# Gated attention, routed experts and a feed-forward in one kernel: scaled keys and weight remainders on GpSimd, the last pair's states ahead of its scores, rows of two batches at other places

## The chip, the cores and the metric

One of the cores of a Trainium2 chip runs the kernel. The metric is the device time of one launch in microseconds (us). The engines are TensorE (PE in the rows; PEld is its weight load), VectorE (DVE), ScalarE (ACT), GpSimd (POOL) and SyncE (SP), which issues most of the transfers. Each works through its own instructions in order and waits for the others by semaphores, so the order in which the program is written is the order on each engine.

## The reference, cut to what matters

```python
for t in range(S):                         # B=4, H=8, S=768, D=48
    state = alpha[:, :, t, :, None] * state + einsum('bhd,bhe->bhde', k[:, :, t], v[:, :, t])
    y[:, :, t] = einsum('bhd,bhde->bhe', q[:, :, t], state)
x = y.transpose(0, 2, 1, 3).reshape(B * S, H * D)         # 3072 rows of 384

logits = x @ w_gate                        # 8 experts
expert_idx = argmax(logits, axis=1)
gate_w = softmax(logits)[arange(N), expert_idx]
for e in range(E):                         # every row goes to one expert
    h = maximum(x[expert_idx == e] @ w1[e], 0.0)          # 384 -> 1024
    out[expert_idx == e] = gate_w * (h @ w2[e])           # 1024 -> 384

h = out @ w_in                             # 384 -> 2048
result = (h * sigmoid(h)) @ w_out          # 2048 -> 384
```

## The kernel before, in words

The kernel has three stages in one launch: the attention with the choice of experts (to about 140 us of the profiled span), the expert layer, and the last feed-forward. Matrix products of the two later stages are made of three, since every operand is split into a rounded high part and a remainder (`wh`, `wl` of a weight slice, `xh`, `xl` of the rows, `hh`, `hl` of the hidden layer).

**Attention.** Two heads make a pair, four pairs a batch row b, so there are pairs p = 0 to 15, and the loop at line 986 has an epilogue p = 16. The sequence is cut in six chunks of 128. Within a chunk the decay is taken out of the recurrence: the queries are multiplied by a running product of alpha, the keys by one from the other end. This preparation runs on "tiles" T = 0 to 12 (with the four pairs of a later batch row packed into three tiles, whose spare rows GpSimd's DMAs gather into the buffer `E_136`, line 518). Its five steps are closures of `prep` (line 525): P_SCAN (`f0`, lines 533 and 536, VectorE), Q_SCALE (line 545, GpSimd for T > 0), DECAY (line 540, ScalarE), R_SCAN (`f1`, line 551, VectorE, into `Rv`, which has one buffer) and K_SCALE (`f2`, line 556, VectorE, reads `Rv`). A table places them: P_SCAN of the tile of pair p at place "scan" of pair p-2, R_SCAN at "end" of pair p-2, K_SCALE at "head" of pair p-1.

A pair itself is: scores of three chunks (line 578, PSUM tile `Ap` in two banks, used again for the other three), the mask (line 583, VectorE, frees `Ap`), keys transposed (line 566, copied to `kst` by ScalarE, line 569), products with the states of the pair before (line 635, tile `Yp`), scores 3 to 5, state updates `U` (lines 590 and 597), the products within the chunks of the pair before (lines 647 and 650, added to `Yp`), the scan over states (`So`, line 607, VectorE), its copies into `Sb` (line 624 ScalarE, 622 VectorE), and copies of `Yp` into `xb` (`y_copy`, line 667 ScalarE, 665 VectorE). `warm(n)` is n products on a tile of zeros (line 506), whose result nobody reads.

**Choice of experts, beside the pairs.** After a batch row, `beside_pairs` (line 920) spreads its routing over the places A, F1, F2, F3, C1 and C2 of the next pairs: logits, `choose` and `weigh` (the gate), `ranks`, `slots`, `digits`, `hots`, `invert`, `add`, which turn the choice into a table of row numbers, and `rows` (line 879), which transposes 128 rows on TensorE, scales them on ScalarE (line 888, tile `xr`, four buffers) and writes them to `x_d` in HBM. The routing of the last batch row cannot hide there: its logits come after pair 15 (line 683, tile `Lp`).

**Expert stage.** The first expert is taken in two parts. Its first 192 rows (`CA`) are gathered from the first three batch rows, so `F1(t)` and `S1(t)` (line 1172 and 1201), t = 0 to 7, run while the routing of the last batch row is done; then the row numbers `gidx` are known (line 842), GpSimd gathers the rest of the rows (line 344), `x_tile` transposes them (line 354) and splits them (lines 356 and 357), and F1 of the second part follows. Between the steps t, the lists `beside` and `between` place the rest of the routing and `rows`. Weight slices arrive by SP (line 319) and are split by `w_split`: ScalarE rounds (`wh`, line 330), VectorE subtracts (`wl`, line 331). All later experts and the last feed-forward follow.

## Time and profile before

| | us |
|---|---|
| median of 3 runs | 793.6 |
| lowest and highest run | 791.74, 795.31 |
| profiled execution | 796.22 |
| its span, first to last instruction | 794.5 |
| PE busy in the span | 768.5 (97%) |
| DVE busy | 479.1 (60%) |
| ACT busy | 358.4 (45%) |
| POOL busy | 147.2 (19%) |

The profiled execution is one run of its own, 2.6 us above the median of the runs; 1.7 us of it lie outside the span. The timeline rows give the start in the span, the duration, the engine and the line; in brackets stands how long the engine was idle before, and what ended that. The windows give the busy time of the engines in stretches and the granted clock of TensorE (1.00 is full speed, 0.50 half).

### The profile page before, as it was taken

The page shows a single profiled execution, that of the slowest core. Times are in us where ns is not written, and L with a number is a line of the kernel's source. Part 1 is how long each engine was busy: PE and PEld are TensorE (multiplying, and loading weights), DVE is VectorE, ACT ScalarE, POOL GpSimd, SP SyncE. Part 2 cuts the span into 40 slices and gives each one's busy share as a digit, 9 for nine tenths or more (in the row PEclk, how much of TensorE's full clock was granted, in tenths as well). Part 3 has the DMA queues.
Part 4 walks back from the last instruction along what each step waited for, and adds up shares of the span by engine and source line. Part 5 has one row for each costly group of instructions (what it writes and reads, how often), then busy time and mean ns, then how long its engine had stood idle before and what let it go on. Part 6 is the DMA issues. An engine that isn't in the chain of part 4 may idle for free.

```text
span 794.5 us, 13324 instructions
## 1 busy us (share of the span) xinstructions
PE 768.5 (97%) x5088; PEld 699.0 (88%) x5088; DVE 479.1 (60%) x825; ACT 358.4 (45%) x680; POOL 147.2 (19%) x194
## 2 busy tenths in 40 slices
PE   7999998899999999999999999999999999999995
PEld 5878877899899999999888999989889988999994
DVE  8989976747788887788688433333433333333332
ACT  2456554425445455556544334453544444333231
POOL 4445321131332231311121200020020011002002
PEclk9899999999999999999999999999999999999998
DMA  9878893433554554555210110031022000001001
GB/s 235 213 181 229 195 268 116 140 115 120 172 170 151 187 186 156 188 179 171 89 60 18 48 45 18 0 93 35 1 75 52 19 11 31 1 1 41 1 1 44
DMA packets 41642, 80.54 MB, mean 101 GB/s; under 512 B 5640, under 2 KB 19863, under 8 KB 41568
## 3 DMA queue, kind: packets, MB, share of 16 engines
q1 hardware_dynamic: 37568, 67.56, 28.9%
q0 software_dynamic: 4000, 12.03, 5.1%
q8 instruction: 42, 0.69, 0.4%
q14 instruction: 32, 0.26, 0.1%
HBM read 68.03 MB, written 9.44 MB: 97 GB/s over the span
## 4 chain that ended last, share of the span: by engine, by line
issue 42%; PE 40%; DVE 5%; DMA 5%; POOL 4%; ACT 2%; SPq 1%; POOLq 0%; DVEq 0%; ACTq 0%
PE hp L1172 16%; PE both L1201 9%; PE yb L1201 4%; POOL out_dram L1386 3%; PE Ap L578 2%; PE both L1367 1%; PE ob L1367 1%; DMA x_d<-xr 1%; PE xt L354 1%; PE Yp L635 1%; DVE Pf L533 1%; PE Yp L650 1%; SPq L437 1%; DMA a__825<-in_alpha_dram 1%; PE Lp L683 1%
## 5 line engine op out<-in xcount | busy, mean ns | idle before, releaser
L1172 PE MATMUL hp<-xh,wh 128*128 128x512 f32 (+9 forms) x504 | 184.7, 369 | 0.1
L1172 PE MATMUL hp<-xh,wl 128*128 128x512 f32 (+9 forms) x504 | 183.7, 368 | 0.8 <-DVE wl L331 0.8
L1346 DVE TENSOR_TENSOR sg<-hp,sg 128x512 f32<-128x512 f32 (+1 forms) x97 | 66.5, 686 | 159.5 <-ACT sg L1345 155.0
L1172 PE MATMUL hp<-xl,wh 128*128 128x512 f32 (+9 forms) x504 | 131.2, 368 | 0.0
L1345 ACT ACTIVATE sg<-hp 128x512 f32<-128x512 f32 (+1 forms) x97 | 57.6, 594 | 156.6 <-PE hp L1172 155.8
L1172 PEld LDWEIGHTS hp<-xh,wh 128*128 128x128 f32 x504 | 94.7, 188 | 10.6 <-issue 0.4
L1172 PEld LDWEIGHTS hp<-xl,wh 128*128 128x128 f32 x504 | 91.7, 188 | 13.9
L1172 PEld LDWEIGHTS hp<-xh,wl 128*128 128x128 f32 x504 | 94.8, 188 | 10.1 <-DVE wl L331 1.0
L1355 DVE TENSOR_TENSOR hl<-sg,hh 128x512 fp32r<-128x512 f32 x95 | 65.8, 692 | 61.8 <-PE ob L1367 41.2
L1354 ACT CAST hh<-sg 128x512 fp32r<-128x512 f32 x95 | 59.0, 621 | 71.1 <-DVE sg L1346 71.1
L1181 ACT ACTIVATE hh<-hp 128x192 fp32r<-128x192 f32 (+8 forms) x72 | 34.5, 479 | 115.2 <-PE hp L1172 113.2
L1386 POOL DMA_INDIRECT out_dram<-o,sidx x24 | 24.2, 1007 | 323.3 <-ACT o L1383 318.6
L1099 POOL TENSOR_TENSOR wl<-dx,wh 128x384 fp32r<-128x384 f32 x32 | 37.9, 1184 | 196.4 <-ACT wh L1096 196.4
L331 DVE TENSOR_TENSOR wl<-raw,wh 128x768 fp32r<-128x768 f32 x64 | 62.1, 972 | 11.4 <-ACT wh L330 10.7
L1367 PE MATMUL both<-wh,hh 128*128 128x384 f32 x190 | 64.4, 339 | 0.0
L1367 PE MATMUL both<-wh,hl 128*128 128x384 f32 x190 | 64.2, 338 | 0.0
L1367 PE MATMUL both<-wl,hh 128*128 128x384 f32 x190 | 64.0, 337 | 0.0
L1367 PE MATMUL ob<-wh,hl 128*128 128x384 f32 x190 | 63.5, 334 | 0.0
L1367 PE MATMUL ob<-wh,hh 128*128 128x384 f32 x190 | 63.5, 334 | 0.0
L1367 PE MATMUL ob<-wl,hh 128*128 128x384 f32 x190 | 63.5, 334 | 0.0
L1183 DVE SCALAR_TENSOR_TENSOR hl<-hp,hh 128x192 fp32r<-128x192 f32 (+8 forms) x72 | 38.9, 540 | 38.7 <-ACT hh L1181 37.5
L330 ACT CAST wh<-raw 128x768 fp32r<-128x768 f32 x64 | 52.9, 828 | 0.3 <-DMA raw<-in_wt_dram 0.3
(359 smaller groups left out, 1464.9 us busy)
## 6 DMA issues: line engine op xcount, KB each, us to landing
raw<-in_wt_dram SPq DMA_DIRECT2D x64, 384.0 KB, 3.2
raw<-in_w_dram SPq DMA_DIRECT2D x32, 384.0 KB, 2.7
raw<-in_alpha_dram SPq DMA_DIRECT2D x16, 336.0 KB, 3.5
x_d<-xr SPq DMA_DIRECT2D x24, 192.0 KB, 2.0
E<-in_q_dram SPq DMA_DIRECT2D x18, 144.0 KB, 4.2
E<-in_k_dram SPq DMA_DIRECT2D x18, 144.0 KB, 3.3
E<-E POOLq DMA_DIRECT2D x18, 114.0 KB
E<-in_q_dram SPq DMA_DIRECT2D x4, 336.0 KB, 10.8
```

Of the source, the lines that this page charges most:

```text
L330: nc.scalar.copy(hi, raw[t])
L331: eng.tensor_tensor(lo, raw.pop(t), hi.bitcast(F32), op=ALU.subtract)
L1099: nc.gpsimd.tensor_tensor(r["lo"], r["x"], r["hi"].bitcast(F32), op=ALU.subtract)
L1172: nc.tensor.matmul(hp, lhsT=a[:, kc * 128 : (kc + 1) * 128], rhs=x[:, kc, c0:c1], start=(i == 0), stop=(i == 8))
L1183: nc.vector.scalar_tensor_tensor(hl[:, :n], in0=hp, scalar=0.0, in1=hh[:, :n].bitcast(F32), op0=ALU.max, op1=ALU.subtract)
L1201: nc.tensor.matmul(yb[dc][:, c0:c1], lhsT=a[:, c : c + 128], rhs=b_[:, : c1 - c0], start=(f == 0 and i == 0), stop=(f == NF - 1 and i == 2),)
L1345: nc.scalar.activation(sg[:, z], hp[:, z], AF.Sigmoid)
L1346: nc.vector.tensor_tensor(sg[:, z], hp[:, z], sg[:, z], op=ALU.mult)
L1354: nc.scalar.copy(hh[:, z], sg[:, z])
L1355: nc.vector.tensor_tensor(hl[:, z], sg[:, z], hh[:, z].bitcast(F32), op=ALU.subtract)
L1367: nc.tensor.matmul(yb[tt], lhsT=a[:, tt * 128 : (tt + 1) * 128], rhs=b_[:, 384:768], start=(f == 0 and i == 0), stop=(f == NF2 - 1 and i = ...
L1386: sc = nc.gpsimd.indirect_dma_start(out=out, out_offset=bass.IndirectOffsetOnAxis(ap=sidx[:, i : i + 1], axis=0), in_=ob, in_offset=None,)
```

## The change

Five places are edited. (1) K_SCALE of the tiles 3 to 6 moves from VectorE to GpSimd. (2) DECAY of tile 1 is issued later in pair 0, and pair 0 ends with 22 products on zeros instead of 6. (3) In pair 14 the rows of the last batch row but one go a place later; the first two weight splits go together to C1 of pair 15, the third to the epilogue, and the remainder of the fourth to GpSimd. (4) In pair 15 the updates and states stand before the scores 3 to 5; a copy of `Yp` of pair 14 moves to VectorE; the transposes of the first gathered tile stand before the last within-products. (5) In the expert stage `ranks`, `slots`, `digits` and `hots` follow the first two `rows` behind F1(2), the other `rows` one step later, two more remainders go to GpSimd, and `x_tile(0, 3)` follows S1(7).

```diff
             def f2():
-                nc.vector.tensor_tensor(
+
+                (nc.gpsimd if 2 < T < 7 else nc.vector).tensor_tensor(
                     s["ks"][:n], s["ks"][:n], chunks(s["Rv"][:n, 1 : SP + 1])[:, :, 1 : CH + 1], op=ALU.mult
...
             c0 = 3 * g * CH
             dst, src = xb[b][:, i, c0 : c0 + 3 * CH], st[p]["y", g].rearrange("p c t -> p (c t)")
-            if p == NP - 1 and g:
+            if p >= NP - 2 and g:
                 nc.vector.tensor_copy(dst, src)
...
                     (p, "C1"): s_["choose"] + s_["weigh"],
-                    (p + 1, "A"): [row[0], row[1]],
-                    (p + 1, "F1"): [row[2]],
-                    (p + 1, "F2"): [row[3]],
+                    (p + 1, "F1"): [row[0], row[1]],
+                    (p + 1, "F2"): [row[2], row[3]],
...
-                    (p + 2, "F1"): [lambda: w_split(0)],
                     (p + 2, "F2"): [invert, add],
                     (p + 2, "F3"): [gather_a],
-                    (p + 2, "C2"): [lambda: w_split(1), lambda: w_split(2), lambda: w_load(4)],
+                    (p + 2, "C1"): [lambda: w_split(0), lambda: w_split(1)],
+                    (p + 2, "C2"): [lambda: w_load(4)],
...
-        for i in (P_SCAN, Q_SCALE, DECAY):
+        for i in (P_SCAN, Q_SCALE):
             f(1, i)
...
             if on:
                 ks_transpose(p, 3, 5)
+            if p == 0:
+                f(1, DECAY)
...
+            if not on:
+                x_rows(XG[0], XS[0], 0, 0, 128, bank(2, [128, KD, 128], "xt"))
+
+            if p == NP - 1:
+                updates(p, 0, 5)
+                states(p)
             if on:
                 for c in range(3, 6):
                     scores(p, c)
+            if p < NP - 1:
                 updates(p, 0, 5)
             if oy:
                 within(p - 1, 0)
                 within(p - 1, 1)
-            if on:
+            if p < NP - 1:
                 states(p)
...
             if p == 0:
-                warm(6)
+                warm(22)
...
             if not on:
-                x_rows(XG[0], XS[0], 0, 0, 128, bank(2, [128, KD, 128], "xt"))
                 x_rows(XG[1], XS[0], 1, 0, CA - 128, bank(0, [128, KD, 128], "xt"))
...
-                w_split(3)
+                w_split(2)
+                w_split(3, nc.gpsimd)
...
         beside = {
-            0: row[0:2],
-            1: row[5:6],
-            2: [last["turns"], invert, add, lambda: gather(0, (1, 2, 3))],
+            1: row[0:2] + [last["ranks"]] + last["slots"] + [digits, hots],
+            2: row[5:6] + [last["turns"], invert, add, lambda: gather(0, (1, 2, 3))],
             6: [lambda: x_tile(0, 1, CA - 128)],
-            7: [lambda: x_tile(0, 2, bk=4), lambda: x_tile(0, 3, bk=3)],
+            7: [lambda: x_tile(0, 2, bk=4)],
         }
...
         for t in range(NF):
-            if t == 1:
-                for f in [last["ranks"]] + last["slots"] + [digits, hots]:
-                    f()
             if t + 1 < NF:
                 F1(t + 1, 0, CA)
+            if t in (0, 2):
+                w_split(t + 3 + (t == 0), nc.gpsimd)
             for f in beside.get(t, []):
                 f()
-            if t in (0, 2, 3, 4):
-                w_split(t + 3 + (t == 0))
+            if t in (3, 4):
+                w_split(t + 3)
             if t >= 4:
                 next_load()
-            S1(t, 0, CA, row[2:5] if t == 0 else [])
+            S1(t, 0, CA, row[2:5] if t == 1 else [])
+        x_tile(0, 3, bk=3)
         F1(*seq[0])
```

VectorE in pairs 2 to 4 before (`a__326` and `a__419` are the alphas of tiles 4 and 5, `E_135` the keys and queries of tile 4; a scan prints as SCALAR_TENSOR_TENSOR):

```order
L551 SCALAR_TENSOR_TENSOR Rv<-a__326,D_0_159 128x774
L583 TENSOR_TENSOR Am<-Ap,mask 128x768
L556 TENSOR_TENSOR E_135<-E_135,Rv 128x768
L533 SCALAR_TENSOR_TENSOR Pf<-a__419,Z_156 128x774
L536 RECIPROCAL D_1_160<-Pf 128x6
L583 TENSOR_TENSOR Am<-Ap,mask 128x768
L607 SCALAR_TENSOR_TENSOR So<-U,E_134 112x288
L551 SCALAR_TENSOR_TENSOR Rv<-a__419,D_1_160 128x774
```

and now (`a__342` and `a__435` are the same two alphas):

```order
L551 SCALAR_TENSOR_TENSOR Rv<-a__342,D_0_159 128x774
L584 TENSOR_TENSOR Am<-Ap,mask 128x768
L533 SCALAR_TENSOR_TENSOR Pf<-a__435,Z_156 128x774
L536 RECIPROCAL D_1_160<-Pf 128x6
L584 TENSOR_TENSOR Am<-Ap,mask 128x768
L608 SCALAR_TENSOR_TENSOR So<-U,E_134 112x288
L551 SCALAR_TENSOR_TENSOR Rv<-a__435,D_1_160 128x774
```

Line 556, the key scaling, is gone from this engine, and the scan of line 551 into `Rv` follows with one mask and one scan in between. It stands on GpSimd, before and now, behind the constants (lines 496 and 498 are their last):

```order
L496 MEMSET keys 128x1
L498 MEMSET caps 1x1 x8
L545 TENSOR_TENSOR E_131<-E_131,Pf 128x768
L545 TENSOR_TENSOR E_132<-E_132,Pf 128x768
L518 DMA E_136<-E_135 16x1824 x2
```

```order
L496 MEMSET keys 128x1
L498 MEMSET caps 1x1 x8
L557 TENSOR_TENSOR E_135<-E_135,Rv 128x768
L545 TENSOR_TENSOR E_131<-E_131,Pf 128x768
L557 TENSOR_TENSOR E_131<-E_131,Rv 128x768
L545 TENSOR_TENSOR E_132<-E_132,Pf 128x768
L557 TENSOR_TENSOR E_132<-E_132,Rv 128x768
L518 DMA E_136<-E_135 16x1824 x2
```

Line 557 is the key scaling there: that of tile 4 (`E_135`) comes behind the constants, and each later one behind the query scaling (line 545) of the tile after it.

VectorE at the last pair before (`E_5_136` belongs to pair 15, `Yp_1946` is the second half of its output, `wl0` to `wl2` are weight remainders):

```order
L583 TENSOR_TENSOR Am_1867<-Ap_1860,mask_163 128x768
L331 TENSOR_TENSOR wl0_97<-raw_1487,wh0_96 128x768
L838 TENSOR_TENSOR tab_108<-tab_108,pt_1880 128x32
L893 TENSOR_SCALAR gidx_a_110<-tab_108 128x2
L894 TENSOR_SCALAR fl_111<-carry_114 1x1
L583 TENSOR_TENSOR Am_1907<-Ap_1900,mask_163 128x768
L607 SCALAR_TENSOR_TENSOR So_1931<-U_177,E_5_136 112x288
L622 COPY Sb_1_162<-So_1931 48x5x48
L331 TENSOR_TENSOR wl1_99<-raw_1489,wh1_98 128x768
L331 TENSOR_TENSOR wl2_101<-raw_1588,wh2_100 128x768
L665 COPY xb_1692<-Yp_1946 112x384
```

and now (`Yp_1906` is the second half of pair 14, `Yp_1960` that of pair 15):

```order
L584 TENSOR_TENSOR Am_1883<-Ap_1876,mask_163 128x768
L839 TENSOR_TENSOR tab_108<-tab_108,pt_1894 128x32
L894 TENSOR_SCALAR gidx_a_110<-tab_108 128x2
L895 TENSOR_SCALAR fl_111<-carry_114 1x1
L608 SCALAR_TENSOR_TENSOR So_1924<-U_177,E_5_136 112x288
L623 COPY Sb_1_162<-So_1924 48x5x48
L584 TENSOR_TENSOR Am_1935<-Ap_1928,mask_163 128x768
L666 COPY xb_1708<-Yp_1906 112x384
L331 TENSOR_TENSOR wl0_97<-raw_1503,wh0_96 128x768
L331 TENSOR_TENSOR wl1_99<-raw_1505,wh1_98 128x768
L357 TENSOR_TENSOR xl0_105<-xt_1964,xh0_104 128x3x128
L666 COPY xb_1708<-Yp_1960 112x384
```

The scan `So` stands before the second mask of the pair, no remainder is left ahead of it, and the two remainders follow behind a copy of pair 14's output.

GpSimd at the start of the expert stage before (`gidx_a` are the row numbers of the first 192 rows, `gidx` those of the rest):

```order
L344 DMA xg_106<-x_d,gidx_a 128x384
L344 DMA xg_107<-x_d,gidx_a 64x384
L344 DMA xg_107<-x_d,gidx 128x384
L344 DMA xg_2025<-x_d,gidx 128x384
L344 DMA xg_2026<-x_d,gidx 64x384
```

and now:

```order
L344 DMA xg_106<-x_d,gidx_a 128x384
L344 DMA xg_107<-x_d,gidx_a 64x384
L331 TENSOR_TENSOR wl_103<-raw,wh_102 128x768
L331 TENSOR_TENSOR wl_2026<-raw,wh_2025 128x768
L331 TENSOR_TENSOR wl_2028<-raw,wh_2027 128x768
L344 DMA xg_107<-x_d,gidx 128x384
L344 DMA xg_2041<-x_d,gidx 128x384
L344 DMA xg_2042<-x_d,gidx 64x384
```

Three weight remainders stand ahead of the gathers of the first expert's other rows.

## Rows read from the trace of the kernel before

**Rows 1.** Busy time of each engine, one stretch; columns: stretch, span, busy, clock, DMA.

```profile
180.00:200.00 20.00, 20.00 (x115) 18.29 (x114) 15.27 (x31) 9.78 (x19) 3.27 (x3) 1.00 0.42 130
```

**Rows 2.** Timeline of TensorE, pairs 0 and 1; start, us, instruction, [idle before, releaser].

```profile
15.28 0.83 PE L506 MATMUL Lw<-wz 128*128 128x256 bf16 x6
18.77 1.65 PE L578 MATMUL Ap<-E 48*128 48x128 f32 x12 [2.65 <-issue]
```

**Rows 3.** TensorE in windows: span, busy, granted clock, DMA share, GB/s.

```profile
19.00:20.00 1.00, 1.00 (x11) 0.50 1.03 277
...
135.00:136.00 1.00, 1.00 (x14) 0.50 0.24 66
143.00:146.00 3.00, 1.65 (x16) 1.00 0.55 202
```

**Rows 4.** Timeline of VectorE, pairs 0 to 6.

```profile
12.63 2.30 DVE L551 TENSOR_TENSOR_SCAN Rv<-a__142,D 112x774 f32<-112x774 f32 x1
...
25.70 0.96 DVE L583 TENSOR_TENSOR Am<-Ap,mask 128x768 f32<-128x768 f32 x1 [1.09 <-PE Ap L578]
...
36.56 0.95 DVE L556 TENSOR_TENSOR E<-E,Rv 128x768 f32<-128x768 f32 x1
37.43 1.76 DVE L533 TENSOR_TENSOR_SCAN Pf<-a__419,Z 128x774 f32<-128x774 f32 x1
...
40.83 1.74 DVE L551 TENSOR_TENSOR_SCAN Rv<-a__419,D 128x774 f32<-128x774 f32 x1
...
43.34 1.48 DVE L556 TENSOR_TENSOR E<-E,Rv 128x768 f32<-128x768 f32 x1
...
53.73 0.96 DVE L583 TENSOR_TENSOR Am<-Ap,mask 128x768 f32<-128x768 f32 x1 [2.12 <-PE Ap L578]
```

**Rows 5.** Timeline of GpSimd, tiles 1 to 5.

```profile
11.66 1.64 POOL L545 TENSOR_TENSOR E<-E,Pf 112x768 f32<-112x768 f32 x1 [7.33 <-DVE Pf L533]
...
40.18 3.82 POOL L545 TENSOR_TENSOR E<-E,Pf 128x768 f32<-128x768 f32 x1
```

**Rows 6.** Instructions of line 545 on GpSimd: count, ns least, median and most.

```profile
L545 POOL TENSOR_TENSOR E<-E,Pf x12: 1625/1637/3822, 11.7 to 103.6; 128x768 f32<-128x768 f32 x9, 112x768 f32<-112x768 f32 x3
```

**Rows 7.** Timeline of ScalarE, pair 14 to the expert stage.

```profile
119.07 0.58 ACT L888 ACTIVATE xr<-Xt,gt 128x384 f32<-128x384 f32 x1 [1.05 <-DMA x_d<-xr]
...
127.06 0.35 ACT L569 COPY kst<-Tp 128x224 f32<-128x224 f32 x1 [0.70 <-PE Tp L566]
...
140.08 0.83 ACT L330 CAST wh<-raw 128x768 fp32r<-128x768 f32 x1
```

**Rows 8.** Timeline of TensorE, pair 15 to the expert stage.

```profile
128.93 0.21 PE L597 MATMUL U<-v__1586,kst 128*48 128x48 f32 x1
...
132.79 1.34 PE L635 MATMUL Yp<-E,Sb 112*112 112x128 f32 x10 [2.33 <-ACT xb L667]
...
137.79 1.95 PE L683 MATMUL Lp<-xb,wgs 112*32 112x256 f32 x24
...
144.56 0.60 PE L885 MATMUL Xt<-ident,xb 112*128 112x112 f32 x4 [1.35 <-ACT xr L888]
```

**Rows 9.** Timeline of VectorE, pair 15 to the second part.

```profile
130.96 0.76 DVE L607 TENSOR_TENSOR_SCAN So<-U,E 112x288 f32<-112x288 f32 x1 [1.41 <-PE Yp L650]
...
140.94 0.96 DVE L331 TENSOR_TENSOR wl<-raw,wh 128x768 fp32r<-128x768 f32 x1 [2.22 <-ACT wh L330]
...
145.73 0.96 DVE L331 TENSOR_TENSOR wl<-raw,wh 128x768 fp32r<-128x768 f32 x1 [0.80 <-ACT wh L330]
...
153.92 0.18 DVE L842 TENSOR_SCALAR gidx<-tt 128x32 uint32<-128x32 f32 x1
...
163.71 0.36 DVE L357 TENSOR_TENSOR xl<-xt,xh 128x192 fp32r<-128x192 f32 x1 [0.47 <-ACT xh L356]
```

**Rows 10.** Timeline of TensorE, end of the expert's first part.

```profile
162.92 0.40 PE L354 MATMUL xt<-ident,xg 64*128 64x64 f32 x3 [0.79 <-DMA xg<-x_d,gidx]
...
164.34 0.30 PE L1172 MATMUL hp<-xh,wh 128*128 128x256 f32 x1
```

More of the change, by code (lines that the diff above doesn't have):

```diff
@@ L1214, in gla_moe_kernel @@
         F1(0, 0, CA)
-        XB[0], XBS[:] = -1, [3, 4, 7, 4, 7, 4, 3, 7, 3]
+        XB[0], XBS[:] = -1, [3, 4, 7, 3, 4, 7, 4, 7, 3]
         digits, hots, invert, add = last_tb
```

## The prediction

> **What bounds the kernel now.** I read the profile from the coarse to the fine: the busy shares in windows, then the timelines of TensorE and VectorE wherever TensorE is not full, then the chain of waits through those places. From about 165 us to the end TensorE is full at the full clock: the window at 180 us shows 20.00 busy of 20 [rows 1]. Nothing of the change lies behind that point. So the edits are worth what they move the start of the second part of the first expert, which before is at 164.34 us [rows 10]; each microsecond there should come out at the end.
>
> In front of that point VectorE sets the pace of the pairs: its timeline has almost no idle time between 15 and 51 us. Its waits stand at few places: 1.09 us before the mask at 25.70 and 2.12 us before the one at 53.73 [rows 4], both for scores. TensorE waits longest before the scores of pair 1, 2.65 us [rows 2], and before the state products of pair 15, 2.33 us [rows 8]. Behind both waits its granted clock is 0.50, the lower of the two levels (1.2 GHz): in the window at 19 us and in the one at 135 us [rows 3]. Behind waits of 1.35 us, as before the transposes at 144.56 [rows 8], it stayed at 1.00, in the window at 143 us [rows 3]. The last piece, from the logits of the last batch row (end 139.74, from 137.79 + 1.95 [rows 8]) to the row numbers (end 154.10, from 153.92 + 0.18 [rows 9]) and to the gathered rows (162.92 [rows 10]), is one chain of small steps.
>
> **The change part by part.** All sums are against the profiled execution, 796.22 us; they are then taken off the median of 793.6, which is 2.6 us lower.
>
> *Products on zeros and DECAY.* Six such products take 0.83 us with their overlap, some 0.107 us each [rows 2]; sixteen more take 1.7 us and lie in TensorE's wait of 2.65 us, so they cost nothing. DECAY no longer stands ahead of the copy of transposed keys on ScalarE, which lets TensorE finish its work of pair 0 some 0.5 us earlier (estimate). The wait shrinks to 2.65 + 0.5 - 1.7 = about 1.5 us. That lies nearer the 1.35 us after which the clock held than the 2.65 us after which it fell. If the clock holds, scores and state products of pair 1 take half as long and the mask at 25.70 no longer waits: 1.1 us gained. If not, 0. Below nothing I see no way, as the zeros end before the scores are released. I take +1.1; what is late next is VectorE itself, without idle time.
>
> *K_SCALE on GpSimd.* It leaves VectorE four times, 0.87 us each from start to start (36.56 to 37.43 [rows 4]). That of tile 6 lies ahead of the 2.12 us wait at 53.73 and is worth nothing; three give 2.6 us. Against this stand three costs. First, GpSimd takes 1.64 us for the same shape where VectorE is not disturbed much, and where both engines read two inputs from SBUF, one of them stretches: the query scaling at 40.18 took 3.82 us, the VectorE scan beside the one at 11.66 took 2.30 instead of 1.74, and a K_SCALE took 1.48 instead of 0.95 [rows 4, 5]. K_SCALE on GpSimd starts when R_SCAN ends; on VectorE one mask follows (some 0.85 us, its 0.96 less the overlap with the next; its other input is in PSUM) and then P_SCAN, which reads two. If it has to stand until GpSimd is done, it loses 1.64 - 0.85 = 0.8 us for each of tiles 3 and 5. Second, R_SCAN writes the only buffer `Rv`, so that of tile T+1 now waits for K_SCALE of tile T on GpSimd; behind that wait on VectorE stand the next mask and P_SCAN, for which the scores and the query scaling wait. For most tiles it is fed in time, some 4 us after the start. But K_SCALE of tile 4 stands behind the constants on GpSimd, which end where the query scaling at 40.18 starts without idle time [rows 5], or some 39.4 with what is gained ahead. It then ends at 41.1 at the earliest, while R_SCAN of tile 5 would be ready at about 40.0 (40.83 less 0.87). That is 1.1 us lost, and 2.7 if the query scaling of tile 5, right behind it, takes another 1.64 us beside it. I take 1.4. Third, nothing else moves on GpSimd's queue but the gathers of spare rows behind K_SCALE of tile 6, which have the slack of pair 5. Sum: 2.6 - 0.8 - 1.4 - 0.8 = -0.4 us. Ends: +1.5 where only the wait behind the constants is paid, and -5.5 as worked out under the slower rival.
> The Trainium skill (GPSIMD Engine Reference, section Key points) says that GpSimd shares its SBUF interfaces with VectorE and that they contend with VectorE instructions that read two SBUF inputs. The trace agrees with it in the 2.30, 1.48 and 3.82 us above, and by that rule alone every P_SCAN here stands; without it, K_SCALE would cost only the wait behind the constants, and part (1) would gain 1.5 us.
>
> *Rows of batch row 2 in pair 14.* The fourth `xr` waits 1.05 us for its buffer, whose transfer lands at 119.07 [rows 7]. Moving rows from place A to F1 and F2 does not move that landing, and the copy of transposed keys still stands behind it on ScalarE. I take 0, with +0.5 and -0.5 as ends.
>
> *The last pair.* Before, `So` starts at 130.96 [rows 9], although the last update had ended at 129.14 (128.93 + 0.21 [rows 8]); then come its copies and the state products at 132.79. Now the updates stand ahead of the scores: the keys are in place at 127.41 (127.06 + 0.35 [rows 7]), TensorE is free of the state products of pair 14 shortly after, and `So` can start at about 128.2. With its copies (the same 1.83 us from 130.96 to 132.79) less the ScalarE copy of pair 14, which no longer stands between, the state products are released at about 130.0. TensorE has scores and the within-products of pair 14 until about 130.3, so the 2.33 us wait is gone and with it the fall of the clock, which made the last within-products, from 134.13 on, run at 0.50. The first transposes of gathered rows come ahead of these products and so fill the wait for the second mask. By the old sequence at full clock the logits end at about 135.6 instead of 139.74: +4.1 us. The two remainders that leave the path of `So` stand behind it and are hidden by the logits. What could be lost: the 1.41 us that `So` waited before is put down to the within-products, for which it has no need; if it were a delay of VectorE that stays, the gain is 2.7.
>
> *Expert stage.* On the chain from the logits to the row numbers the first hidden layer now stands on ScalarE behind the rounding of two slices instead of one: 0.8 us lost (0.83 at 140.08 [rows 7]). Three remainders of 1.64 us or more on GpSimd meet VectorE's small steps with two inputs; at worst 4.9 us, at best 0; I take 3.5 from the places where they fall. Two remainders leave VectorE, which stood in the chain at 140.94 and 145.73 [rows 9], 0.87 us each; and of the wait of 0.80 us at the latter I count 0.5 as gone. 0.8 + 3.5 - 1.75 - 0.5 = 2.05 us longer. The row numbers come 4.1 - 2.05 = 2.05 us earlier, at 152.05. The gathers follow with 8.8 us (154.10 to 162.92) as before; GpSimd's remainders are done by then. At the end S1(7) now lies in the wait for the last gathered tile (1.0 us off the path, 163.32 to 164.34), but the splitting of that tile is no longer hidden by it: about 0.7 (a wait of 0.47 and 0.36 at 163.71, less overlap [rows 9]). So the second part starts at 152.05 + 8.8 + 0.4 + 0.7 = about 161.95 instead of 164.34: +2.4 for the last pair and the expert stage together, with ends +4.5 (GpSimd disturbs nothing) and +1.0 (it holds every step).
>
> Sum: 1.1 - 0.4 + 0 + 2.4 = 3.1 us. 796.22 becomes 793.1 in a profiled execution, and the median 790.5.
>
> **The rivals.**
> *The two engines seldom meet* (masks and waits for TensorE lie beside GpSimd's work): K_SCALE gives +1.5 instead of -0.4, the remainders take 2 us instead of 3.5 in the chain, 6.5 in all: 787.1. For it speaks that the median of GpSimd's twelve query scalings is 1637 ns, so that most ran undisturbed [rows 6]; against it, that K_SCALE always starts one mask ahead of a scan with two inputs.
> *The clock still falls in pair 1, and GpSimd holds the chain of the routing to the full*: -1.1, -1.4: 793.0. For it, 1.5 us lies between the waits that the trace shows; against it, it is close to the shorter ones.
> *Slower: R_SCAN waits for K_SCALE.* If K_SCALE on GpSimd is stretched as the query scaling at 40.18 was, that of tile 4 runs from 40.2 to 44.0 and R_SCAN of tile 5, ready at 40.0, loses 4.0 us; that of tile 6 then finds K_SCALE of tile 5 behind another stretched query scaling and loses 1.7; with three stalls of P_SCAN of 0.8 that is 8.1 against 2.6 removed, -5.5. With 1.1 and 2.4 gained it leaves 2.0 us lost: 795.6. It decides from a loss of 3.5 us in that place on. Against it, the median of the twelve query scalings is 1637 ns and the longest 3822 [rows 6].
> *The change doesn't do what it says:* `So` keeps its stall, the rows stay with their transfer and the routing eats the rest: 793.6.
>
> **How the numbers follow.** Forecast 790.5 with chance 0.45 (its own range 788 to 792.8); engines seldom meeting 787.1 with 0.20; clock and routing 793.0 with 0.20; slower 795.6 with 0.10; no effect 793.6 with 0.05. A change below 0.5%, here 4.0 us, can't be told from none by a measurement of this kernel (the three runs before lie 3.6 us apart): faster is below 789.6, slower above 797.6. Of the forecast case a third falls below 789.6 and of the second nearly all: 0.15 + 0.19, with a little of the third 0.38. Above 797.6 lies half of the slower case and a little more: 0.06. The rest, 0.56, is within. The range 786.5 to 794.8 leaves out half of the slower case and the outer ends of the others.
>
> **What would show it.** Clock 1.00 in the windows from 19 to 25 us and no wait at the second mask of pair 1 (right), or 0.50 again (wrong). P_SCAN of tiles 4 and 6 some 0.8 us longer or later, and a wait of VectorE for GpSimd before R_SCAN of tile 5 only. `So` of pair 15 at about 128 less what is gained before, clock 1.00 at 135 us, logits ending 4 us earlier. Row numbers only 2 us earlier, with stretched small steps beside GpSimd's remainders. The forecast is wrong if R_SCAN waits at several tiles, or if the gathers and not the routing end the first part.

## The result, and the profile after

The change made the kernel slower: median 799.89 us in 14 runs (796.79 to 806.63) against 793.49 in 14 runs of before (791.74 to 795.90), a ratio of 1.0085, 95% interval 1.0065 to 1.0104. The forecast was 790.5 with a range from 786.5 to 794.8. The profiled execution of the changed kernel has a span of 799.5 us, 5.0 more than before.

Four marks cut the span into pieces that can be compared: the second mask of pair 14 (VectorE), the copy of the last logits (ScalarE), the row numbers (VectorE) and the first product of the second part (TensorE). Before, the first two are these (the other two are in [rows 9] and [rows 10]):

```profile
121.28 0.96 DVE L583 TENSOR_TENSOR Am<-Ap,mask 128x768 f32<-128x768 f32 x1 [1.38 <-PE Ap L578]
```

```profile
139.81 0.37 ACT L697 COPY l<-Lp 96x256 f32<-96x256 f32 x1 [1.59 <-PE Lp L683]
```

After, VectorE from pair 1 to the row numbers:

```profile
24.98 0.96 DVE L584 TENSOR_TENSOR Am<-Ap,mask 128x768 f32<-128x768 f32 x1 [0.19 <-PE Ap L579]
...
29.05 2.59 DVE L533 TENSOR_TENSOR_SCAN Pf<-a__342,Z 128x774 f32<-128x774 f32 x1
...
40.48 3.18 DVE L551 TENSOR_TENSOR_SCAN Rv<-a__435,D 128x774 f32<-128x774 f32 x1 [1.20 <-POOL E L557]
...
44.44 2.61 DVE L533 TENSOR_TENSOR_SCAN Pf<-a__554,Z 128x774 f32<-128x774 f32 x1
...
54.27 0.96 DVE L584 TENSOR_TENSOR Am<-Ap,mask 128x768 f32<-128x768 f32 x1 [2.98 <-PE Ap L579]
...
123.28 0.96 DVE L584 TENSOR_TENSOR Am<-Ap,mask 128x768 f32<-128x768 f32 x1 [1.47 <-PE Ap L579]
...
140.78 1.25 DVE L745 TENSOR_TENSOR df<-lg,mx 128x48 f32<-128x48 f32 x1
...
143.57 1.73 DVE L725 TENSOR_TENSOR oh<-w,fi 128x48 bf16<-128x48 f32 x1
...
151.88 1.70 DVE L860 TENSOR_TENSOR turn<-rk,iota_f 128x64 f32<-128x64 f32 x1
...
155.53 0.18 DVE L843 TENSOR_SCALAR gidx<-tt 128x32 uint32<-128x32 f32 x1
```

TensorE in the expert stage:

```profile
145.37 0.20 PE L756 MATMUL pp<-oh,tri 128*128 128x48 bf16 x1 [1.88 <-DVE oh L725]
...
162.14 0.53 PE L354 MATMUL xt<-ident,xg 128*128 128x128 f32 x3 [2.08 <-DMA xg<-x_d,gidx]
...
168.23 0.58 PE L1180 MATMUL hp<-xh,wh 128*128 128x256 f32 x1 [0.41 <-ACT xh L356]
```

| piece of the span, us | before | forecast | after |
|---|---|---|---|
| to the second mask of pair 14 | 121.28 | 120.6 | 123.28 |
| from there to the copy of the logits | 18.53 | 14.4 | 14.90 |
| from there to the row numbers | 14.11 | 16.2 | 17.35 |
| from there to the second part | 10.42 | 10.1 | 12.70 |
| from there to the end | 630.16 | 630.16 | 631.27 |

Each entry is the difference of two of these starts (the copy of the logits after starts at 138.18, the last row of the next fence). The last pair did nearly what was forecast, 3.6 us gained; everything else lost, 8.6 us together. The last two rows of the table, behind the row numbers, hold 3.4 us that no term of the sum had. Their cause is in the windows of TensorE (columns: span, busy, granted clock, DMA share, GB/s):

```profile
147.00:149.00 2.00, 2.00 (x14) 0.59 0.35 124
...
164.00:166.00 2.00, 1.46 (x7) 0.61 0.35 105
166.00:168.00 2.00, 1.82 (x10) 0.50 0.30 78
```

Behind the wait of 1.88 us for the one-hot table, and behind those of 2.08 and 0.89 us for gathered rows, the granted clock falls to 0.50, the lower of the two levels (1.2 GHz); 0.59 and 0.61 are windows in which it changes. Both falls come some 2 us after the longer wait has ended. Before, neither stretch had a fall. In the last pair, where before had one [rows 3], there is none now. In pair 1, where before had another, it still falls, only later:

```profile
21.00:22.00 1.00, 1.00 (x6) 0.54 1.03 249
22.00:23.00 1.00, 1.00 (x7) 0.50 1.05 260
```

In front, K_SCALE runs on GpSimd, the gathers of spare rows follow it, and ScalarE waits 3.51 us for the transfer of an xr in pair 8 (timelines of GpSimd and of ScalarE):

```profile
38.79 1.66 POOL L557 TENSOR_TENSOR E<-E,Rv 128x768 f32<-128x768 f32 x1
40.41 1.62 POOL L545 TENSOR_TENSOR E<-E,Pf 128x768 f32<-128x768 f32 x1
...
52.15 3.19 POOL L518 DMA_DIRECT2D E<-E  x6
```

```profile
77.10 0.58 ACT L889 ACTIVATE xr<-Xt,gt 128x384 f32<-128x384 f32 x1 [3.51 <-DMA x_d<-xr]
...
138.18 0.37 ACT L698 COPY l<-Lp 96x256 f32<-96x256 f32 x1 [1.56 <-PE Lp L684]
```

R_SCAN of tile 5 waits 1.20 us for K_SCALE of tile 4 and then takes 3.18 us beside GpSimd's query scaling; two P_SCANs take 2.59 and 2.61 instead of 1.76. From the second mask of pair 1 to that of pair 5 VectorE needs 29.29 us (24.98 to 54.27) instead of 28.03 (25.70 to 53.73 [rows 4]): 1.3 us lost, in spite of 2.6 us of work taken away. That repeats: this piece takes 27.95 to 28.03 us in 14 of the 15 profiles of this document with K_SCALE on VectorE (29.18 in e6, where the clock stays low longer), and 29.26 to 30.16 in the five with it on GpSimd. The whole front does not repeat so well: the second mask of pair 14 comes between 120.05 and 123.70 us in the profiles with K_SCALE on VectorE and four xr buffers, so the 2.0 us lost there in the table are not all the change's.

### The profile page after: what moved, and what is told of

The parts are those of the page before. It is cut to its first block, busy times and chain, and to the rows that moved or that the text cites. A ratio compares the mean times of both kernels' runs of the same rounds, so it can differ in the third digit from the quotient of the medians.

```text
span 799.5 us, 13365 instructions
## 1 busy us (share of the span) xinstructions
PE 771.9 (97%) x5104; PEld 702.9 (88%) x5104; DVE 480.2 (60%) x819; ACT 358.0 (45%) x679; POOL 157.4 (20%) x201
## 5 line engine op out<-in xcount | busy, mean ns | idle before, releaser
L331 DVE TENSOR_TENSOR wl<-raw,wh 128x768 fp32r<-128x768 f32 x61 | 59.2, 972 | 8.9 <-ACT wh L330 7.9
```

Source lines behind the costliest of these rows:

```text
L331: eng.tensor_tensor(lo, raw.pop(t), hi.bitcast(F32), op=ALU.subtract)
```

## The experiments

The experiments were measured in groups (e1 to e4; e5, e6 and the two second profiles; e7 to e10; f; g), on different chips of one kind. The kernel before itself has medians of 793.5 to 797.1 us in them, so each ratio is taken to before in the same group. Between groups a ratio can differ too: e3 has 1.0004 and 0.9985, the kernel of e9 and f1 has 0.9954 and 0.9932. The changed kernel was measured ahead of all groups, so that differences to its 1.0085 carry that uncertainty of some 0.002. First all of them, then each with its edit.

| kernel | ratio to before | 95% interval |
|---|---|---|
| changed kernel | 1.0085 | 1.0065 to 1.0104 |
| e1 keys back on VectorE | 1.0041 | 1.0018 to 1.0064 |
| e2 splits back on VectorE | 1.0018 | 0.9996 to 1.0039 |
| e3 both back | 1.0004 | 0.9987 to 1.0021 |
| e3 again | 0.9985 | 0.9964 to 1.0005 |
| e4 before, keys on GpSimd | 1.0018 | 0.9997 to 1.0039 |
| e5 changed, clock held | 1.0023 | 1.0006 to 1.0040 |
| e6 before, new last pair | 0.9982 | 0.9962 to 1.0002 |
| before again | 1.0011 | 0.9988 to 1.0035 |
| e7 before, six xr | 1.0016 | 0.9995 to 1.0036 |
| e8 e3, zeros before the gathered rows | 0.9986 | 0.9969 to 1.0003 |
| e9 e8, six xr | 0.9954 | 0.9935 to 0.9974 |
| e10 before, pair 1 alone | 1.0006 | 0.9987 to 1.0025 |
| f1 e9 again | 0.9932 | 0.9911 to 0.9952 |
| f2 f1, splits on GpSimd | 0.9977 | 0.9959 to 0.9995 |
| f3 f1, keys on GpSimd | 0.9963 | 0.9942 to 0.9985 |
| f4 f1 without zeros | 0.9980 | 0.9961 to 1.0000 |
| g1 f1, old last pair | 0.9948 | 0.9923 to 0.9974 |
| g2 f1, old pair 1 | 0.9944 | 0.9918 to 0.9969 |

**One part undone, or alone (e1 to e4).** e1 has the first edit, e2 the second, e3 both, in the changed kernel; e4 is the kernel before with the first edit the other way.

```diff
-                (nc.gpsimd if 2 < T < 7 else nc.vector).tensor_tensor(
+                nc.vector.tensor_tensor(
...
-                w_split(3, nc.gpsimd)
+                w_split(3)
...
-                w_split(t + 3 + (t == 0), nc.gpsimd)
+                w_split(t + 3 + (t == 0))
```

e1. Expected: 

> The changed kernel with K_SCALE of all tiles on VectorE again. Theory: K_SCALE on GpSimd holds back the gathers of spare rows that stand behind it on GpSimd's queue (first one at 52.15 us instead of 48.20), the loads behind them land about 3 us later, and ScalarE waits 3.51 us instead of 0.97 for an xr buffer in pair 8; undone, that wait falls to about 1 us and the median falls from 799.9 by 2 to 3 us, to about 797.4; the routing stays as slow as in the changed kernel. Rival: K_SCALE costs only the direct stretch of scans and the 1.20 us wait of R_SCAN, and the gathers don't matter: the wait in pair 8 stays near 3.5 us and the median is about 799.4.

e2. Expected: 

> The changed kernel with the three weight remainders on VectorE instead of GpSimd, at the same places of the program. Theory: beside GpSimd's remainders three small steps of the routing stretch (0.21 to 1.25, 0.32 to 1.73, 0.23 to 1.70 us), TensorE waits for them and its clock falls in 147 to 150 and 164 to 170 us; without them the steps are short, the clock stays at 1.00 and the median falls by 4 to 6 us, to 794 to 796. Rival: the loss comes from the new order of ranks and rows on TensorE and ScalarE; the median stays at 798 to 800.

e3. Expected: 

> The changed kernel with both K_SCALE and the weight remainders on VectorE; the last pair, DECAY, the products on zeros and the order of the expert stage as changed. Theory: both losses go, the gain of the last pair (about 3.5 us) and of pair 1 (0.7 us) stays: about 790.5, below the kernel before. Rival (the new order of the expert stage costs by itself): 795 to 797.

e4. Expected: 

> The kernel before with nothing changed but K_SCALE of tiles 3 to 6 on GpSimd. Theory: 1 to 3 us slower than before (794.5 to 796.5), with the gathers starting near 52 us and a wait of ScalarE of some 3.5 us for an xr buffer in pair 8. Rival (only the direct stretch matters): within 0.5 us of before and the wait in pair 8 near 1 us. The forecast's own term was 0.4 us lost.

Measured: e1 797.75, e2 794.36, e3 793.93, e4 795.92 us, with before at 793.95. So the splits cost most (0.0067 of the ratio, 5.3 us, from e2 to the changed kernel; 0.0037 from e3 to e1, whose intervals just overlap), the keys less (0.0044 from e1 to the changed kernel, 0.0014 from e3 to e2, 0.0018 alone in e4), and without both the kernel is where before was. In e2 the three steps of the routing have their old lengths:

```profile
140.45 0.21 DVE L745 TENSOR_TENSOR df<-lg,mx 128x48 f32<-128x48 f32 x1
...
142.21 0.32 DVE L725 TENSOR_TENSOR oh<-w,fi 128x48 bf16<-128x48 f32 x1
...
149.38 0.23 DVE L860 TENSOR_TENSOR turn<-rk,iota_f 128x64 f32<-128x64 f32 x1
```

e1 tells the steps from the clock. Its steps are stretched as in the changed kernel and TensorE waits 1.86 us for the one-hot, but this time the clock stayed up there, and fell only behind the gathered rows:

```profile
142.41 1.74 DVE L725 TENSOR_TENSOR oh<-w,fi 128x48 bf16<-128x48 f32 x1
...
152.94 0.18 DVE L843 TENSOR_SCALAR gidx<-tt 128x32 uint32<-128x32 f32 x1
```

```profile
143.00:145.00 2.00, 0.71 (x7) 1.00 0.71 263
145.00:147.00 2.00, 2.00 (x22) 1.00 0.03 9
...
162.00:164.00 2.00, 2.00 (x12) 0.50 0.25 78
```

From the logits (137.02) to the row numbers it needs 15.92 us, against 14.45 in e3's profile and 17.35 in the changed kernel: 1.5 us for the stretched steps, net of what left VectorE, and 1.4 more where the clock fell. The expectation of e3, 790.5, failed: its first profile was 4.6 us shorter than that of before, its median not. And the theory of e1 and e4 that the delayed gathers of spare rows (52.15 instead of 48.20) make ScalarE wait in pair 8 fell: e1, with the gathers at 48.20 again, waits 2.14 us there for the transfer, and e8 below, with them at 47.67, 2.70. The wait of 2.33 us that e4 has there, with the gathers late, the trace puts down to TensorE.

**The clock held (e5).** Products on zeros where TensorE waited, in the changed kernel: 40 in `ranks`, ahead of its first product, and 24 in `x_tile`, ahead of the first transposes of the rows gathered by `gidx`.

```diff
+                for _ in range(40 if b == B - 1 else 0):
+                    nc.tensor.matmul(pp, lhsT=wz[:, 0:128], rhs=wz[:, 0:64], start=True, stop=True)
...
+                for _ in range(24 if (e, kt) == (0, 1) else 0):
+                    nc.tensor.matmul(xt[:, 0, :], lhsT=wz[:, 0:128], rhs=wz[:, 0:128], start=True, stop=True)
```

Expected: 

> The changed kernel with 40 products on zeros (64 columns) ahead of the first product of ranks, where TensorE waited 1.88 us for the one-hot, and 24 (128 columns) ahead of the first transposes of gathered rows, where it waited 2.08 us. The waits for data stay, the idle time goes. Theory (TensorE's idle time behind GpSimd's remainders lets the clock fall, which costs some 4 us in 147 to 151 and 164 to 170 us): the granted clock stays at 1.00 in both stretches and the median falls from 799.9 to about 796. Rival (the stretched steps and the late gathers are the cost, the clock only follows): the median stays within 1.5 us of 799.9, because the second part of the expert still waits for the gathers.

Measured 798.74 us, ratio 1.0023 instead of 1.0085: 4.9 us back, though the one-hot comes no sooner (7.12 us after the copy of the logits starts, in both profiles). The clock is 1.00 where it had fallen:

```profile
147.00:149.00 2.00, 1.89 (x20) 1.00 0.29 104
...
164.00:166.00 2.00, 1.86 (x15) 1.00 0.36 101
```

The pieces of its profile fit: 15.92 us for the routing instead of 17.35, 10.70 instead of 12.70 to the second part, 630.06 instead of 631.27 behind it, 4.6 us together. Some 0.5 us of these need not be the clock's: the gathered rows came 6.1 us after the row numbers instead of 6.6. So most of the loss is the clock, and the wait is its occasion. In absolute terms the median lies within the rival's 1.5 us of 799.9, but before has 796.91 us in this group; by the ratio the rival is out.

**The last pair alone, and second profiles (e6).** e6 is the kernel before with the edits of `y_copy`, of pair 15's order and of the splits at C1 and C2 (the third and fourth part of the change without `rows` and GpSimd).

```diff
...
+            if p == NP - 1:
+                updates(p, 0, 5)
+                states(p)
             if on:
                 for c in range(3, 6):
                     scores(p, c)
...
```

e6. Expected: 

> The kernel before with the last pair's part alone: updates and states ahead of the scores 3 to 5, the copy of pair 14 on VectorE, the first transposes ahead of the within-products, and the weight splits behind; no GpSimd, no rows moved, the expert stage as before. Forecast term: So at about 128.2 us, logits 4 us earlier, no fall of the clock at 135 us; median 3 to 4 us below before (790 to 791). Rival (the wait and the fall of the clock in the profile of before are not in most of its runs, or the gain is given back in the routing): the median within 1 us of before, with logits early but the second part of the expert no earlier than in the typical run of before.

Before again. Expected: 

> The kernel before, unchanged, for a second profile. The profiled execution read for the forecast took 796.22 us, 2.3 us above the median of 35 runs (793.95). Theory: a typical execution starts the second part of the expert near 162 us instead of 164.34, because one of the two falls of the clock (pair 1, last pair) or a late transfer is absent; the time behind that point is 630 us as before. Rival: the front is the same and the spread lies behind 165 us.

e3 again. Expected: 

> The same kernel as e3_both_back, for a second profile: its first one (791.72 us) was the fastest of its 12 runs, 2.2 us under their median. Theory: a typical execution starts the second part near 162 us instead of 159.72, with either a fall of the clock or a longer wait for an xr transfer that the first profile did not have. Rival: the front is as in the first profile and the spread lies behind it.

Measured: e6 796.11 (before 796.91), a gain of 1.4 us by the ratio, at an interval from 3.0 us to none, not 4.1. In its profile the clock falls in the expert stage, behind a wait of 1.02 us for gathered rows (0.58 in the window at 164 us), so that the second part starts 11.35 us after the row numbers instead of 10.42; a part of what the last pair gains can be lost there again. The second profile of before, on another chip, has the same span, 794.5, and the second part at 164.37: the first one was no single accident. But in profiles of other kernels whose last pair is written as before, that piece is shorter: 15.52 us in e4, 17.18 in e7 and 17.91 in e10, against 18.53 and 18.67 in before. In e4 `So` follows the mask without the wait of 1.41 us that it had before, and the clock does not fall:

```profile
131.94 0.96 DVE L583 TENSOR_TENSOR Am<-Ap,mask 128x768 f32<-128x768 f32 x1 [0.65 <-PE Ap L578]
132.81 0.75 DVE L607 TENSOR_TENSOR_SCAN So<-U,E 112x288 f32<-112x288 f32 x1
```

In the new order the piece is 14.9 to 15.9 us in all profiles. What the edit takes away is thus not in each execution; what makes `So` wait in some of them the runs don't show. The second profile of e3 shows the other side of its 4 us: it waits 1.08 us for gathered rows, less than the 1.23 of its first one, and this time, with one more wait of 0.54 us, the clock falls behind it, so that the second part starts at 163.83 instead of 159.72 (of which 2.1 us stood before):

```profile
158.15 0.52 PE L354 MATMUL xt<-ident,xg 128*128 128x128 f32 x3 [1.08 <-DMA xg<-x_d,gidx]
```

```profile
160.00:162.00 2.00, 1.80 (x9) 0.57 0.40 108
```

**Transfers, zeros and pair 1 (e7 to e10).** e7 changes one number in the kernel before; e8 is e3 with the second loop of e5; e9 has both; e10 is before with DECAY behind the second transposes and `warm(22)`.

```diff
-            xr = xp.tile([128, 4, 2, D], F32, tag="xr", name="xr", bufs=4)
+            xr = xp.tile([128, 4, 2, D], F32, tag="xr", name="xr", bufs=6)
```

e7. Expected: 

> The kernel before with six xr buffers instead of four. In the profiles ScalarE waits 0.8 to 3.5 us in pair 8 for the transfer of an xr that still holds a buffer, in kernels with the same program up to there. Theory A (that wait is a cause of the spread of the front): it goes, and the median falls by 0.5 to 2 us. Theory B (the next transfer or VectorE takes over): within 0.5 us of before.

e8. Expected: 

> e3_both_back with 24 products on zeros ahead of the first transposes of gathered rows. Theory: an earlier routing lets TensorE reach that place sooner and wait 1.1 to 1.2 us there for the gather; in one of the two profiles its clock then fell, and the second part began 4 us later (163.83 against 159.72, 2.1 of which stood before). Held, the median is 2 to 3 us below before (ratio about 0.997). Rival: the products on zeros only lengthen TensorE's own queue; no change against e3_both_back (ratio 0.999 to 1.000).

e9. Expected: 

> e8_back_hold with six xr buffers. If both terms hold, about 1 us less than e8_back_hold, ratio about 0.996 against before; if the buffers are worth nothing, as e8_back_hold.

e10. Expected: 

> The kernel before with DECAY of tile 1 behind the second transposes of pair 0 and 22 products on zeros instead of 6, nothing else. Forecast term: 1.1 us gained at the second mask of pair 1 and carried to the end, ratio 0.9986. Rival: in two profiles of the kernel before that mask starts at 25.70 and 25.16 us, and the second part of the expert at 164.34 and 164.37, so what is gained in pair 1 is lost again at a later transfer or wait: ratio 1.000, and the second part of the expert within 0.3 us of 164.35.

Measured: e7 797.34, e8 795.55, e9 792.70, e10 797.45, before 797.05. e8 does not differ from e3 (1.0004 and 0.9985) by more than the intervals. e10 is what the forecast's first term needed, and it gives nothing. Its profile shows where the gain goes: in pair 8 it is still ahead (second mask of pair 9 at 80.92 instead of 81.81, and 81.28 in the second profile of before), but in pair 11 ScalarE waits for the transfer that holds an xr buffer. In the eight profiles with four buffers in which ScalarE comes to it at 102.4 us or earlier, this transfer ends between 103.2 and 105.7; the two that come earliest, e3 at 99.9 and e10 at 100.5, have it at 104.0 and 105.0. e10, then before:

```profile
104.96 0.58 ACT L888 ACTIVATE xr<-Xt,gt 128x384 f32<-128x384 f32 x1 [4.51 <-DMA x_d<-xr]
```

```profile
104.58 0.58 ACT L888 ACTIVATE xr<-Xt,gt 128x384 f32<-128x384 f32 x1 [2.64 <-DMA x_d<-xr]
```

e3's waits 4.09 us there, to 104.02. Behind this wait e10 loses more: TensorE waits 0.74 and 1.05 us for the copies of `Yp` that the logits of batch row 2 read, its clock falls, as it does not there in before, and the next mask comes at 113.57 instead of 111.59:

```profile
108.00:110.00 2.00, 1.86 (x9) 0.55 1.05 252
```

With six buffers the waits for the transfer are gone (e7, e9); alone that moves nothing that can be measured, with e8's zeros it is worth 0.0032, with intervals that just overlap. Why e7 alone gains nothing stays open.

**One move put back into the fastest kernel (f1 to f4).** f1 is e9. f2 has `nc.gpsimd` for the three splits again, f3 for K_SCALE, f4 leaves the zeros out.

f1. Expected: 

> The same kernel as e9_back_hold_xr6 (everything on VectorE again, products on zeros ahead of the gathered rows' transposes, six xr buffers), as the yardstick of this call: ratio about 0.9955 against before.

f2. Expected: 

> The yardstick with the three weight remainders on GpSimd, nothing else. Theory: three small steps of the routing stretch by 3.9 us together (1.04 + 1.41 + 1.47), two remainders of 0.87 us leave VectorE, TensorE waits about 1.9 us for the one-hot and its clock falls behind that: row numbers 1 to 2 us later, second part 3 to 4 us later than in the yardstick, ratio about 1.000. Rival (the loss seen before came from transfers and chance): ratio within 0.001 of the yardstick.

f3. Expected: 

> The yardstick with K_SCALE of tiles 3 to 6 on GpSimd, nothing else. With six buffers no wait of ScalarE for x_d can swallow the difference. Theory: R_SCAN of tile 5 waits 1.2 us and is stretched to 3.2, two P_SCANs are stretched by 0.8, 2.6 us leave VectorE: the second mask of pair 5 and all behind it 1.5 to 2 us later, ratio about 0.9975. Rival (the forecast's term of 0.4 us or less): ratio within 0.001 of the yardstick.

f4. Expected: 

> The yardstick without the 24 products on zeros. Theory: in about half of the executions the clock falls behind the 1.1 to 1.2 us wait for the gathered rows and costs 2 us: ratio 0.9965 to 0.998, with a wider spread. Rival: the products on zeros do nothing: ratio as the yardstick.

Measured: f1 791.64, f2 794.88, f3 793.21, f4 794.74, before 796.51. The splits on GpSimd cost 0.0045 (3.6 us), with intervals that do not overlap; the keys 0.0031 (2.5 us), with intervals that overlap; the zeros are worth 0.0048 (3.8 us), with intervals that do not. f2's profile has the whole chain, the stretched one-hot and the fall of the clock behind it, and its routing takes 17.54 us (135.00 to 152.54) against f1's 14.31:

```profile
140.40 1.73 DVE L725 TENSOR_TENSOR oh<-w,fi 128x48 bf16<-128x48 f32 x1
...
152.54 0.18 DVE L843 TENSOR_SCALAR gidx<-tt 128x32 uint32<-128x32 f32 x1
```

```profile
143.00:145.00 2.00, 2.00 (x12) 0.50 0.02 6
```

f3's profile shows the stretched scan of tile 5 again, without a wait before it. Its front is late by 1.38 us for an alpha transfer that f1 didn't wait for, so that the loss in this profile is not the keys' alone:

```profile
42.39 3.18 DVE L551 TENSOR_TENSOR_SCAN Rv<-a__435,D 128x774 f32<-128x774 f32 x1
```

f4 waits 1.32 us for gathered rows, as e3 did. In this profile the clock held and the second part comes 10.55 us after the row numbers (f1: 10.48); in the median of its runs 3 us are lost. That the clock falls in those is likely by e3's second profile, but no profile of f4 shows it.

**The two gains, in the fastest kernel (g1, g2).** g1 takes the last pair's edits out of f1, g2 those of pair 1.

g1. Expected: 

> f1_best_again with the last pair as before (updates and states behind the scores, the copy of pair 14 on ScalarE, the transposes behind the within-products, the splits at their old places). Forecast term: 4.1 us lost again, ratio about 0.998. From the profiles: the last pair took 18.5, 18.7, 17.9, 17.2 and 15.5 us from the second mask of pair 14 to the copy of the logits in the old order, 14.9 to 15.9 in the new one, so about 2 us are lost on the mean: ratio about 0.996.

g2. Expected: 

> f1_best_again with DECAY of tile 1 and the products on zeros of pair 0 as before. Forecast term: 1.1 us lost. With six xr buffers no wait of ScalarE at 104 us takes the early gain back: ratio 0.0010 to 0.0014 above f1_best_again's. Rival: the loads take it back as in e10_pair1, no difference.

Measured: g1 792.92, g2 791.81, before 796.10. Neither differs from f1 and e9 (0.9932 and 0.9954) by more than the intervals. g1's profile has the old last pair in full, 18.77 us with the clock at 0.50, but its routing is 0.85 us shorter (13.46), since one of the splits no longer stands in it: the net of the two is 2.3 us in that profile, and in the median less than can be told. g2's second mask of pair 1 is at 24.51 us, no later than f1's at 24.83, although its clock falls in that pair (0.50 in the window at 20 us): that profile has nothing to lose there.

f1 is below before, 0.9932 (0.9911 to 0.9952), and as e9 0.9954; the changed kernel had 1.0085. It keeps the changed kernel's order of the last pair and of the expert stage, everything on VectorE, with 24 products on zeros and six xr buffers.

## Why the prediction was wrong, point by point

*The step that failed* is the expert stage's, where it says: "Three remainders of 1.64 us or more on GpSimd meet VectorE's small steps with two inputs; at worst 4.9 us, at best 0; I take 3.5". The mechanism came as written: the three steps stretched by 1.04, 1.41 and 1.47 us, 3.9 together. The net of the remainders' move, 3.5 less 1.75 and 0.5 in the forecast, is 1.5 us where the clock holds (e1 against e3), and the routing then takes 15.92 us (e1, e5) where 16.2 was forecast. So this sum was right. What the step left out is the next link, a term taken at nothing without a reason: a stretched step makes TensorE wait, and the clock falls behind the wait. That costs 1.4 us in the routing, up to 2.0 to the second part and 1.2 behind it, which e5 gave back. The forecast priced the clock in pair 1 and in the last pair, and took it to be 1.00 from there on. By the medians the forecast is missed by 9.5 us (3.1 gained was forecast, 6.4 lost measured). The clock behind the expert stage's waits is about half of it (e5: 4.9); the rest is roughly the two gains that did not reach the end, 2.7 us of the last pair (e6) and 1.1 of pair 1 (e10), and 1 to 2 us of K_SCALE.

*K_SCALE on GpSimd*: right in its parts, mis-sized in sum. The stalls of P_SCAN were forecast at 0.8 each and measured at 0.83 and 0.85; the wait of R_SCAN at 1.1, measured 1.20. But R_SCAN behind the wait was stretched by 1.44 as well, and the forecast took 1.4 for both together. Net -1.3 us in the profile instead of -0.4; f3 and e4 measure 2.5 and 1.4 us lost, with wide intervals. The scan beside the query scaling, which ends at 42.03 us, ends 1.63 us behind it at 43.66, and the scan alone takes 1.74: it stood nearly until the other had ended. The Trainium skill (GPSIMD Engine Reference, section Key points) says that GpSimd shares its SBUF interfaces with VectorE and contends with VectorE instructions that read two SBUF inputs; these rows agree.

*The sentence on the gathers behind K_SCALE* ("which have the slack of pair 5") can't be called wrong: they went 4 us later, and nothing in the runs ties a cost to it.

*Products on zeros in pair 1*: wrong in the changed kernel's profile, in part right elsewhere. TensorE's wait shrank to 1.65 us (1.5 was forecast), but the clock still fell to 0.50 behind it, the sign that the prediction had named for being wrong. The second mask waits 0.19 us there instead of 1.09, but so it does in the second profile of before, without the edit. Over all profiles the clock falls in all six with the old pair 1 and in six of the 14 with the new one; in e10 it holds. That the 1.1 us reach the second part was wrong too: e10 loses them at the transfer near 104 us and behind it. g2, with six buffers, shows no loss beyond the intervals either, and there no such wait takes anything back; the term's size stays open.

*Rows in pair 14*: 0 was taken, and the wait of the fourth xr is still there (0.79 us after); no run took it apart.

*The last pair*: 4.1 forecast, 3.6 in the profile, with no fall of the clock. But part of it is not in every execution of before; e6 measured 1.4 us.

*The rivals*: the slower one had R_SCAN waiting, the right place and the wrong size (1.20 us, not 5.7); the larger loss lay elsewhere. Of the rival at 793.0 both conditions came nearly true, the fall of the clock in pair 1 and the routing held, and it was still 7 us short, since it too had no clock behind the stretched steps. That the engines seldom meet is out.

## What to carry to other kernels

Price a wait of TensorE by what its clock does behind it, not by its length: the first product of the second part took 0.58 us at a granted clock of 0.50 and 0.30 before at 1.00. Products on zeros in the wait gave that back (e5) although the one-hot came no sooner. Work moved to GpSimd is not free for VectorE: look which two-input instructions of VectorE run beside it, and who waits for those. And don't count a gain ahead of a wait for a transfer until the transfer is seen to move with it.

## What the runs showed of the hardware that was not expected

The same wait doesn't always bring the same clock. Behind 1.86 to 1.88 us without a product the clock fell in the changed kernel and in f2 and stayed at 1.00 in e1. Behind waits of 1.23 and 0.38 us for gathered rows it stayed in e3's first profile, and behind 1.08 and 0.54 us it fell in its second. In the two profiles of before it fell behind the same wait of pair 1 (2.65 and 2.66 us), in one at once (0.72 in the window at 18 us), in the other only at 21 us (0.69). The Trainium skill (TensorE: Matmul & The Clock Gate, section Part 1: The HAM clock gate) says of the rise of the clock at the start of a kernel that its point varies from run to run; these profiles show the same of a fall.

A VectorE step with two inputs beside a GpSimd product of 1.8 us took 1.25 to 1.74 us instead of 0.21 to 0.32. In the changed kernel the three steps end 0.07 to 0.17 us after the product beside them, so each stood until the product was done.
